# An attention and highway kernel whose engine orders come from a list instead of from ranks

## The chip, the cores and the metric

The kernel runs on one core of a Trainium2 chip. The metric is the device time of one execution in microseconds (us); the time of a kernel is the median of several runs.

## What is computed

Eight batches of twelve heads, 448 positions, 64 values a head. q and k are divided by their norms, scores are their products over tau = 0.1, a softmax follows, and the result weights v. The heads side by side are the 3584 x 768 input of a highway layer.

```
q_n = q / (norm(q) + 1e-6);  k_n = k / (norm(k) + 1e-6)
attn = softmax(q_n @ k_n.T / tau)
x = (attn @ v), heads side by side          # 3584 x 768
H = relu(x @ w_h);  T = sigmoid(x @ w_t + b_t)
out = T * H + (1 - T) * x
```

## The kernel before, in words

**The work.** A unit of attention is a *pair* of heads (n = 0 to 47, six pairs a batch); a unit of the highway layer is a *tile* of 128 rows (m = 0 to 27, three tiles a batch and a fourth for every second batch, made of what is left over of two). Each step of a pair or tile is an operation with a name, and the texts here use these names:

- `lk`, `lq`, `rk`, `rq`, `v`, `x`, `w`: loads of k, q (the main part, and the rest of 64 positions), of v (main part and rest) and of the weights. All are DMAs issued by POOL (L542 to L580, L493), and they convert to 16 bits. `f` is the first q and k, from the SP and ScalarE queues.
- `sq`, `f1`, `f2`, `red`, `nw`: squares of q and k (L602 on ScalarE or L603 on VectorE), their sums, and the inverse root in Newton steps (L631 to L636).
- `nm`: the normalised q and k of a pair, in two halves, on POOL or VectorE (L663).
- The transposed pair comes either by TensorE (`pt`, L678) and a copy (`cp`, on ScalarE L687 or VectorE L689), or by one DMA transpose on SP (`tr`, L694). 14 pairs take the first way and 34 the second.
- `qk`: scores in four parts (L734, L737), into two PSUM buffers `sc` in turn and one `sl`. `ex`: their exponentials on ScalarE (L751, L753).
- `vc`: copies of v into its padded form `vp` (ScalarE L710, VectorE L711). Two buffers `vf` hold the raw v, so the load of batch b waits for the four `vc` of batch b - 2.
- `av`: the weighted sums (L774) and `un`: the division by the sums (L782 to L788), into `xb`, and into `st` for the left-over rows, which `sh` moves to `xl` by DMA on SP.
- `xp` and `xc`, or `xt`: the transposed tile, by TensorE and a copy or by DMA on SP (10 and 18 tiles).
- `ff`: the four products of a tile (L859, bias L862). `d`, `t`, `g`, `h`, `e`, `o` are the tile's elementwise steps on VectorE and ScalarE, the last add `o` on VectorE or POOL (L946). `st0` to `st27` are the stores on SP, from three buffers.

Three PSUM buffers `pb` serve transposes, weighted sums and products alike.

**The order.** The kernel builds a list of these operations, each with the engines it may run on and a cost for each, with what it depends on, the buffers it takes and gives back. `Planner.plan` then walks through a model of time: whenever an engine is free, it takes, among the operations that are ready, the one of the lowest *step*, and so fixes engine and order. The steps are not those written beside the operations: a list `RANKS` with one number for each operation replaces them (a thousandth of the number is the step). TensorE prefers to stay with scores, or with the other matmuls, by 1.5 steps; switching costs 97 ns in the model. A load is taken only if no load of a lower step is ready. Two more lists are given: `HOLDS` says behind the scores of which pair each load is released, and `CHOICES` which of the two ways of transposing is taken. The result is a fixed instruction order for each engine. On the chip each engine works its own list from the front and waits by semaphores for what the others owe it.

[...]

The lines that pick an operation, and those that apply the lists:

```
for op in ready[e]:
    if op.when[e] > now:
        continue
    if op.dma is not None:
        if op.dma[0] == "load" and (deep or op.step > first):
            continue
...
for op, rank in zip(P.ops, RANKS, strict=True):
    op.step = rank / 1000.0
```

Of the kernel before, what the change touches and what calls it, by code (L numbers as in the profile page):

```python
# [19 lines left out]
RANKS = [  # L20
    -335, -1932, -1271, 3133, 2841, 5167, 5173, 1697, -74, 6773, 6082, 5915, 5667, -1915, -723, -495, -2732, 1644, 620, -269, 42,
    2265, -1441, -1744, 2062, 2152, -918, 3256, 2331, 4414, 3785, 5845, 5519, 4272, 2090, 6377, 10666, 9870, 9695, 10058, 9508,
    5134, 10049, 12769, 9902, 11732, 9552, 15932, 12758, 13944, 12583, 17233, 17256, 18670, 16784, 21822, 21777, 17890, 16690,
    20295, 25563, 25092, 13883, 20180, 25169, 26082, 23748, 29102, 29384, 27764, 26341, 29412, 32284, 33661, 37263, 31791, 33122,
    37907, 38585, 33898, 39108, 35328, 36704, 2394, 857, 4933, 3498, 4444, 6285, 10703, 11593, 10638, 11144, 8739, 13218, 20655,
    13960, 15171, 13417, 14400, 25150, 20593, 18723, 28847, 29728, 21766, 25308, 35536, 28630, 30992, 34871, 37517, 38415, 50453,
    45614, -1615, 1033, 685, 27, 6016, 2128, -2432, 7156, -451, -321, 1859, 3036, 2762, -1404, -5331, 5658, 8169, 4881, 6526, 927,
    11947, 3192, 4533, 3266, 11318, 7906, 9123, 8750, 15817, 13133, 9488, 11519, 13103, 13084, 13298, 13103, 15254, 13703, 13892,
    24037, 17015, 13938, 20089, 20295, 18477, 24447, 22187, 22773, 25024, 22713, 22339, 22443, 26082, 28086, 27444, 27656, 29034,
    30771, 33015, 30877, 32139, 37989, 38621, 34820, 33021, 38290, 32551, 35641, 33263, 34723, 40989, 42110, 38461, 33253, 44252,  # L30
    43633, 45447, 35798, 44076, 3231, 2565, -1751, 1566, 9632, 4904, 1466, 6198, 7375, -98991, 4914, 5920, 2537, 7720, -465, 1383,
    5460, 6251, 5748, 29126, 4663, 5087, 4744, 9779, 9843, 6545, 5105, -30262, -37170, 7855, 5855, 10788, 5142, 11144, 85225,
    8540, 7641, 9742, 4465, -114808, 7028, 11341, 12462, 7201, -37464, 10316, 9159, 13329, 10032, -121016, 12706, 8421, -78332,
    -5590, 13447, 8378, 9045, 10097, 12946, -121346, 12211, 12981, -91454, -98771, 19451, 15028, 12867, -105710, 14573, 18844,
    11133, 14125, -23135, -44370, 20938, 16676, 16656, -31575, -163611, 22258, 16377, 14459, 21437, -115592, 18504, 16397, 14004,
    13897, -88475, 19773, 16898, 18256, 57676, -91195, 15754, 19706, 22628, 22205, 21596, 10816, 18889, 18282, 201292, 45600,
    21254, 19936, 13867, 25179, -28175, 24642, 18088, 20941, -16514, 59267, 20464, 17361, 20075, 23083, 20381, -175770, 27216,
    27122, 181487, 114978, 25193, 24125, 25084, -39395, -94136, 25227, 25049, 23771, 30866, 27677, 1440, 21856, 26649, 20642,
    -93406, 25116, 22457, 23353, -5592, -73152, 27038, 25127, 26246, 26984, 28561, -147028, 33880, 30995, 68610, 33770, 31413,
    31877, 30222, -79746, 83829, 33050, 29574, 34024, 112191, 33698, 35292, 32513, 31456, -1565, 55132, 31620, 29222, 30471, 6683,  # L40
    38178, 32009, 28869, 29922, 31584, 32695, 36344, 39730, 40450, 106424, 239806, 36530, 39625, 43884, -33467, 104089, 37075,
    35523, 38187, -11090, -64566, 36130, 37728, 34352, -81003, -138719, 39693, 36458, 32804, 63129, 123831, 39266, 37892, 33195,
    108295, 133523, 37203, 45017, 41083, 41355, 108347, 44744, 40273, 39414, 11515, 194501, 41016, 41953, 42696, 48735, 37150,
    41422, 40336, 41702, 162857, 55277, 45550, 41590, 41916, 103590, 149762, 39797, 43288, 42467, 81073, 82634, 41132, 6839, 7350,
    8242, 6304, 14280, 10159, 13740, 10591, 18303, 14858, 11534, 13430, 24113, 22797, 19366, 21837, 19098, 24269, 26279, 25213,
    29363, 34108, 37459, 31510, 32869, 37287, 35777, 36518, 46146, 45644, 43305, 43543, -1403, 4599, -991, -288, 198, 4194, 3309,
    9036, 6978, 4679, 6017, 7165, 3946, 6351, 3005, 4829, 6519, 3682, 8257, 4979, 8964, 5934, 5252, 2718, 9743, 7885, 7346, 7454,
    6624, 9536, 966, 6752, 8008, 9328, 7610, 6383, 2346, 4401, 6111, 8198, 11578, 9204, 10485, 8362, 9755, 2989, 6805, 3222, 9770,
    5763, 6413, 8303, 8981, 6853, 6631, 6857, 11857, 8358, 10504, 8417, 9866, 5189, 8798, 9553, 9916, 12186, 13302, 10953, 9638,
    15284, 8840, 11922, 5831, 10408, 6315, 9449, 5527, 4622, 12082, 16809, 8219, 8672, 10011, 8092, 7049, 11942, 11705, 11157,  # L50
    12832, 15876, 7930, 9895, 9099, 5712, 10667, 13770, 11844, 9866, 11844, 12801, 10128, 15457, 14600, 15312, 14139, 17140,
    10136, 15238, 14468, 13703, 15449, 13977, 10994, 10023, 12308, 12009, 12223, 14945, 12406, 16825, 15267, 14102, 15635, 14144,
    13172, 13358, 17103, 14232, 14643, 13449, 14221, 14378, 13744, 19613, 16238, 15619, 14766, 22292, 19045, 18526, 10880, 15482,
    17749, 18298, 15280, 18728, 17528, 12279, 19524, 20449, 17979, 15834, 18591, 18055, 18938, 17702, 17919, 18780, 21066, 22200,
    19537, 14358, 18187, 22934, 19437, 18287, 21567, 15623, 20390, 21595, 17459, 16669, 17661, 17250, 18895, 16286, 18854, 20586,
    21181, 21955, 21362, 21923, 21688, 17683, 24823, 21763, 19818, 17894, 19658, 22713, 22147, 21948, 21075, 25045, 16800, 24464,
    23733, 21929, 23853, 26560, 18284, 23132, 21813, 21733, 23445, 18280, 24449, 19741, 21846, 22733, 26683, 20892, 25039, 25991,
    22326, 25330, 23979, 25318, 26442, 26729, 24225, 19280, 22262, 22552, 22093, 22645, 23788, 23923, 26924, 28536, 22788, 21384,
    23795, 22599, 26462, 27417, 26160, 25941, 24071, 26999, 25952, 25184, 27650, 31212, 27018, 26947, 28061, 27536, 28032, 29925,
    23838, 31447, 25659, 28699, 24777, 30028, 31103, 29120, 32621, 32372, 27439, 26006, 28909, 29374, 29530, 29088, 29914, 24681,  # L60
    31528, 35518, 28197, 30867, 29458, 32059, 28431, 31586, 27901, 29414, 31676, 35932, 29300, 36310, 32645, 31589, 30167, 38648,
    31605, 30849, 31730, 27814, 29997, 28249, 31468, 33782, 30279, 31438, 31179, 29456, 32630, 31483, 34201, 31369, 34151, 31355,
    34669, 33889, 36281, 32831, 36426, 35943, 30241, 30471, 30218, 31940, 36522, 35571, 35198, 32061, 36043, 35685, 34551, 34481,
    35120, 36994, 34447, 34944, 36601, 38422, 36822, 32448, 35295, 32369, 37188, 35896, 35002, 38841, 35936, 39091, 38774, 39560,
    34045, 32204, 32951, 32981, 35956, 33750, 37119, 37830, 35133, 34557, 37647, 37806, 38233, 40428, 36896, 38364, 36625, 39199,
    37755, 34740, 37385, 40737, 37549, 37703, 38412, 35577, 36947, 38983, 38392, 42624, 40461, 43990, 38941, 40965, 36940, 40435,
    42631, 39576, 39905, 42465, 39599, 39033, 40762, 40160, 43447, 43685, 39785, 38249, 42821, 40891, 39347, 43595, 41144, 45787,
    41272, 46121, 42659, 49862, 43166, 42012, 38517, 43507, 42102, 43711, 45454, 45152, 44045, 47521, 43039, 44021, 37849, 44344,
    38023, 38673, 32560, 39755, 37139, 39384, 39438, 43664, 44903, 46532, 45791, 52656, 44070, 49771, 40817, 48013, 44821, 49369,
    38608, 45378, 44257, 46036, 45379, 48187, 44122, 49724, 46123, 48526, 39822, 44757, 43950, 42745, 41717, 45307, 41257, 43609,  # L70
    49107, 46378, 42257, 43967, 41895, 44075, 42503, 46864, 46654, 51736, 48408, 49869, 47400, 50799, 45287, 48998, 45566, 51428,
    46465, 56278, 49246, 52417, 46119, 50866, 47960, 48731, 49000, 47578, 47435, 50129, 48381, 48080, 9319, 20240, 20022, 27086,
# [115 lines left out]
class Planner:  # L188
# [18 lines left out]
    def add(self, name, engs, *a, **k):  # L207
        op = Op(name, engs, *a, **k)
        op.seq = len(self.ops)
        self.ops.append(op)  # L210
        return op

    def plan(self):
        ready = {e: [] for e in ENGINES}
        self.ops = [op for op in self.ops if op.var is None or self.choices[op.var[0]] == op.var[1]]
        used = set(self.ops)
# [18 lines left out]
        mode, now = None, 0.0  # L235
# [800 lines left out]
```

## Time and profile before

| What | Value |
|---|---|
| median of five runs | 286.02 us (284.08 to 287.7) |
| the profiled execution's own time, and its span | 284.38 us, 282.6 us |
| mean granted TensorE clock | 0.956 |
| busy: TensorE, VectorE, ScalarE, POOL | 246.1, 221.9, 206.7, 130.4 us |
| transposes of q and k by DMA | 34, median 4.8 us to landing |

The span goes from the first to the last instruction; the execution's own time is 1.8 us longer. Busy times are sums over the whole span. A row of the timeline or of the waits names the line of the kernel, the operation and the tile written and read (`sc<-qkT` are scores from the transposed pair); what stands behind the arrow in brackets is what ended the idle time before it. TensorE's matmuls overlap in the pipeline, so a row's duration is longer than its share of the engine's time: a part of scores of four matmuls occupies TensorE for about 0.19 us, a weighted sum of 32 matmuls for 1.01, a product of six for 0.97 and one of seven with the bias for 1.14.

### The profile page before, as it was taken

To read this page: it belongs to the slowest core of one execution; us is meant where nothing else is said; L and a number is where in the kernel's file an instruction comes from. 1 tells how busy PE (TensorE), PEld (TensorE's weight loads), DVE (VectorE), ACT (ScalarE), POOL (GpSimd) and SP (SyncE) were. 2 spreads that over 40 slices of the span, in tenths; PEclk is the share of its full clock that TensorE was granted. 3 is DMA by queue.
4 is the path that set the end of the run, shared out by engine and by line. 5 is a ranking of instruction groups with operands and counts; after the bars stand their busy time and mean duration, and the time that the engine had idled before them with its cause. 6 is when DMAs were issued, how large, how long until landed. Compare 5 with 4: busy or idle time off the path is not lost.

```text
span 282.6 us, 7727 instructions
## 1 busy us (share of the span) xinstructions
PE 246.1 (87%) x3103; PEld 149.5 (53%) x3103; DVE 221.9 (79%) x512; ACT 206.7 (73%) x286; POOL 130.4 (46%) x170
## 2 busy tenths in 40 slices
PE   5218778999979699999998999799999999999991
PEld 1105546447635367655754566356665654676560
DVE  4588678769979977898959999599688996557663
ACT  2376986999977657999589689578899699482140
POOL 8968325766655544368570676642232240002000
PEclk9555979999999999999999999999999999999999
DMA  8999999999789999989699999999989788414823
GB/s 126 157 162 163 203 170 129 104 156 199 91 139 155 166 211 189 194 113 145 158 206 187 114 231 156 168 168 145 190 184 111 109 141 168 118 58 99 144 116 106
DMA packets 109942, 42.75 MB, mean 151 GB/s; under 512 B 103249, under 2 KB 106321, under 8 KB 109906
## 3 DMA queue, kind: packets, MB, share of 16 engines
q0 software_dynamic: 57696, 18.65, 65.5%
q1 hardware_dynamic: 51762, 23.38, 43.0%
q8 instruction: 24, 0.39, 0.6%
q10 hardware_dynamic: 448, 0.23, 0.3%
q14 instruction: 12, 0.10, 0.1%
HBM read 37.75 MB, written 11.01 MB: 173 GB/s over the span
## 4 chain that ended last, share of the span: by engine, by line
PE 56%; DMA 15%; DVE 8%; POOL 7%; ACT 6%; issue 6%; SPq 0%; DVEq 0%; ACTq 0%; POOLq 0%
PE pb L859 27%; PE pb L774 14%; PE sc L734 9%; DMA qkT<-qkn 8%; ACT ex L751 3%; DMA raw<-in_q_dram 3%; PE sl L737 3%; PE pb L862 2%; DMA raw<-in_k_dram 2%; POOL qkn L663 2%; POOL raw L560 2%; PE pb L678 2%; DMA vf<-in_v_dram 2%; POOL raw L545 1%; DVE sq L603 1%
## 5 line engine op out<-in xcount | busy, mean ns | idle before, releaser
L751 ACT ACTIVATE ex<-sc 128x896 f16<-128x896 f32 x144 | 127.3, 929 | 25.9 <-PE sc L734 25.0
L859 PEld LDWEIGHTS <-xT 128*128 128x128 f16 x672 | 61.1, 98 | 52.3 <-issue 15.0
L663 POOL TENSOR_TENSOR qkn<-raw,rs 128x448 f16<-128x448 f16 x43 | 39.8, 937 | 55.0 <-DVE rs L636 26.2
L734 PE MATMUL sc<-qkT 64*64 64x448 f16 x576 | 50.6, 378 | 15.4 <-ACT ex L751 7.1
L859 PE MATMUL pb<-w_t,xT 128*128 128x384 f16 x336 | 64.0, 327 | 0.0
L859 PE MATMUL pb<-w_h,xT 128*128 128x384 f16 x336 | 61.3, 327 | 0.9 <-DVE d L877 0.8
L774 PEld LDWEIGHTS <-ex 128*128 128x128 f16 x1536 | 53.5, 99 | 11.4 <-issue 8.2
L774 PE MATMUL pb<-vp,ex 128*128 128x65 f16 x1536 | 56.9, 195 | 1.8 <-ACT ex L751 0.7
L734 PEld LDWEIGHTS <-qkT 64*64 64x64 f16 x576 | 15.5, 106 | 36.8 <-issue 22.0
L877 DVE SCALAR_TENSOR_TENSOR d<-pb,xb 128x384 f16<-128x384 f32 x48 | 26.3, 554 | 10.9 <-PE pb L859 9.7
L663 DVE TENSOR_TENSOR qkn<-raw,rs 128x448 f16<-128x448 f16 x51 | 31.9, 664 | 0.0
L753 ACT ACTIVATE ex<-sl 128x448 f16<-128x448 f32 x48 | 26.8, 559 | 2.9 <-PE sl L737 2.9
L784 DVE TENSOR_TENSOR xb<-pb,rd 128x384 f16<-128x384 f32 x48 | 26.8, 558 | 1.7
L885 ACT ACTIVATE t<-pb 128x384 f16<-128x384 f32 x30 | 14.8, 500 | 11.1 <-PE pb L862 11.0
L885 ACT ACTIVATE pb<-pb 128x384 f32<-128x384 f32 x26 | 12.9, 498 | 13.3 <-PE pb L862 13.2
L946 POOL TENSOR_TENSOR o<-d,xb 128x768 f32<-128x768 f16 x6 | 9.8, 1636 | 27.7 <-DVE d L938 21.0
L602 ACT ACTIVATE sq<-raw 128x2688 f16<-128x2688 f16 x9 | 22.0, 2452 | 0.6 <-DMA vf<-in_v_dram 0.6
L917 DVE SCALAR_TENSOR_TENSOR pb<-pb,d 128x384 f32<-128x384 f32 x26 | 14.6, 562 | 6.8 <-ACT pb L885 6.8
L782 DVE RECIPROCAL rd<-pb 128x7 f32<-128x7 f32 x48 | 9.7, 201 | 10.9 <-PE pb L774 10.5
L862 PE MATMUL pb<-brow,ones 128*128 128x384 f16 x56 | 18.3, 326 | 0.0
L610 DVE TENSOR_TENSOR f<-sq 128x1344 f16<-128x1344 f16 (+2 forms) x17 | 14.6, 872 | 4.6 <-ACT sq L602 4.5
L737 PE MATMUL sl<-qkT 64*64 64x448 f16 x96 | 18.0, 362 | 0.1
(69 smaller groups left out, 265.3 us busy)
## 6 DMA issues: line engine op xcount, KB each, us to landing
out_dram<-o SPq DMA_DIRECT2D x24, 384.0 KB, 3.8
vf<-in_v_dram POOLq DMA_DIRECT2D x16, 288.0 KB, 6.4
raw<-in_k_dram POOLq DMA_DIRECT2D x14, 288.0 KB, 6.7
raw<-in_q_dram POOLq DMA_DIRECT2D x14, 288.0 KB, 7.3
out_dram<-o SPq DMA_DIRECT2D x8, 192.0 KB, 2.9
w_t<-in_moe_w_t_dram POOLq DMA_DIRECT2D x2, 576.0 KB, 8.8
w_h<-in_moe_w_h_dram POOLq DMA_DIRECT2D x2, 576.0 KB, 14.3
vp<-in_v_dram POOLq DMA_DIRECT2D x16, 48.0 KB, 4.7
```

What stands on the lines that cost most here:

```text
L602: return nc.scalar.square(o, r)
L663: return eng.tensor_mul(qkn_r[n][:, :, g, :], raw_r[b][:, 42 * g + 7 * hn : 42 * g + 7 * hn + 7], rs_r[b][:, g, h].unsqueeze(2).to_broadca ...
L734: last = nc.tensor.matmul(sc_r[n, j][o, g, 0:S], lhsT=T[:, 128 * j + 64 * i : 128 * j + 64 * i + 64], rhs=rhs, start=True, stop=True)
L737: nc.tensor.matmul(sl_r[n][r, 0:S], lhsT=T[:, 832:896] if g == 0 else T[:, 384:448], rhs=rhs, start=True, stop=True)
L751: nc.scalar.activation(o, sc_r[n, j][:, :, 0:S], AF.Exp, scale=inv_tau / (NSC * NSC))
L753: nc.scalar.activation(ex[:, 3136 : 3136 + S], sl_r[n][:, 0:S], AF.Exp, scale=inv_tau / (NSC * NSC))
L774: nc.tensor.matmul(u[:, s * 65 : s * 65 + 65], lhsT=l, rhs=r, start=(m == 0), stop=(m == len(ms) - 1))
L784: nc.vector.tensor_tensor(out=xo, in0=u[:, 0:6, 0:D].rearrange("p (g i) e -> p g i e", g=2), in1=rd[:, 0:6].rearrange("p (g i) -> p g i", ...
L859: nc.tensor.matmul(pt[:, 0:MH], lhsT=xT[:, c, :], rhs=w_sb[w][:, c, ms], start=(c == 0), stop=(w == 0 and c == CC - 1))
L862: nc.tensor.matmul(pt[:, 0:MH], lhsT=ones[:, :], rhs=brow[:, ms], start=False, stop=True)
L877: nc.vector.scalar_tensor_tensor(out=d_r[m][:, h], in0=pb_r[m, w, h][:, 0:MH], scalar=0.0, in1=xsrc()[:, ms], op0=ALU.max, op1=ALU.subtract)
L885: nc.scalar.activation(src if flat else t_r[m][:, h], src, AF.Tanh, scale=0.5)
```

## The change

`RANKS` goes. In its place stands `QUEUES`: for each of the five engines the numbers of the operations that it runs, in the order in which it runs them. The planner gets this list. It sets each operation to the one engine whose list names it, and in its walk through time an engine may take nothing but the front of its list, even if other operations are ready; the rule that a load waits for loads of lower steps does not apply. What the walk still decides are the buffers (which of two or three, by the model's times) and the order in which the instructions are written down. `HOLDS` has new numbers. `CHOICES`, the costs, the operations and all shapes are as before. The list was found by small moves, each judged by the end of the plan in the model.

```
-RANKS = [
-    -335, -1932, -1271, 3133, 2841, 5167, 5173, 1697, -74, 6773, 6082, 5915, 5667, -1915, -723, -495, -2732, 1644, 620, -269, 42,
...
-]
+QUEUES = {
+    "PE": [
+        1, 196, 466, 468, 470, 472, 201, 476, 478, 216, 480, 211, 506, 482, 496, 498, 206, 500, 474, 502, 486, 484, 488, 490, 492,
...
+    ],
...
+}
...
-    def plan(self):
+    def plan(self, queues=None):
...
+        if queues is not None:
+            for e in ENGINES:
+                for op in queues[e]:
+                    op.engs = {e: op.engs[e]}
+            queues = {e: list(reversed(queues[e])) for e in ENGINES}
...
-                    if op.when[e] > now:
+                    if op.when[e] > now or (queues is not None and op is not queues[e][-1]):
                         continue
                     if op.dma is not None:
-                        if op.dma[0] == "load" and (deep or op.step > first):
+                        if queues is None and op.dma[0] == "load" and (deep or op.step > first):
                             continue
...
+                if queues is not None:
+                    queues[e].pop()
...
-    for op, rank in zip(P.ops, RANKS, strict=True):
-        op.step = rank / 1000.0
...
+    queues = {e: [P.ops[i] for i in QUEUES[e]] for e in ENGINES}
...
-    order = P.plan()
+    order = P.plan(queues)
```

In operations, the fronts of TensorE's two lists read (`qk1_2` is part 2 of pair 1's scores, `ff2_00` the first product of tile 2):

```
before: fill pt0 qk0_0 qk0_1 qk0_2 qk0_3 pt1 qk1_0 qk1_1 pt4 pt3 pt2 qk1_2 qk1_3 qk4_0 av0 qk3_0 av1 qk3_1 ...
after:  fill pt0 qk0_0 qk0_1 qk0_2 qk0_3 pt1 qk1_0 qk1_1 pt4 qk1_2 pt3 qk4_0 qk1_3 qk3_0 qk3_1 pt2 qk3_2 av0 ...
```

and those of SP's:

```
before: bld f tr5 xt1 sh0 st0 st1 tr12 xt4 sh1 tr13 tr14 xt6 tr16 tr17 st2 tr15 tr18 st3 tr20 tr21 st4 tr22 ...
after:  bld f tr5 xt1 tr12 tr13 tr17 xt4 tr14 st0 sh0 st1 tr16 tr15 sh1 st2 xt6 tr18 tr20 tr21 tr22 xt7 sh2 ...
```

## The prediction

> **What bounds the kernel now.** I read the summary first, then the time cut into stretches of 20 us, then the waits, then TensorE's and ScalarE's timelines where the waits are long. The page's summary and slices:
>
> ```profile
> PE 246.1 (87%) x3103; PEld 149.5 (53%) x3103; DVE 221.9 (79%) x512; ACT 206.7 (73%) x286; POOL 130.4 (46%) x170
> ...
> PE   5218778999979699999998999799999999999991
> ...
> PEclk9555979999999999999999999999999999999999
> ```
>
> TensorE carries the kernel. Its idle time is at the front: slices 1 to 6 are thin, and the granted clock is half there. The stretches (start:end, length, then busy time and count of PE, PEld, DVE, ACT, POOL, then clock, DMA share, GB/s) say how the load is spread:
>
> ```profile
> 20.00:40.00 20.00, 13.70 (x198) 9.30 (x199) 15.38 (x34) 16.11 (x20) 9.37 (x13) 0.76 1.39 174
> 40.00:60.00 20.00, 18.50 (x234) 11.19 (x231) 15.19 (x39) 16.50 (x24) 15.19 (x19) 0.94 1.33 128
> 60.00:80.00 20.00, 17.05 (x278) 11.48 (x276) 18.69 (x45) 19.01 (x23) 11.82 (x15) 1.00 1.20 147
> 80.00:100.00 20.00, 17.39 (x165) 8.91 (x166) 17.52 (x35) 13.80 (x20) 11.88 (x14) 1.00 1.18 162
> 100.00:120.00 20.00, 19.73 (x321) 13.13 (x320) 15.52 (x36) 15.54 (x24) 7.90 (x9) 1.00 1.38 199
> ...
> 240.00:260.00 20.00, 20.00 (x296) 13.63 (x295) 11.84 (x32) 10.68 (x17) 2.34 (x2) 1.00 0.35 86
> ```
>
> After 100 us TensorE is full but for a few us; between 60 and 80 ScalarE (19.01 of 20) and VectorE (18.69) are nearly as full. An order can win only what TensorE idles. The waits of TensorE and its weight loads:
>
> ```profile
> PEld L734 <- DMA qkT<-qkn: 8.0, 6, 2.1
> PE sc L734 <- ACT ex L751: 7.1, 9, 2.4
> PE sc L734 <- DMA qkT<-qkn: 6.1, 4, 2.0
> ```
>
> So what an order can repair is in two places: scores waiting for exponentials, nearly all before 40 us, and scores waiting for a DMA transpose of q and k. The four transposes are these (TensorE's timeline; idle before in brackets):
>
> ```profile
> 80.11 0.57 PE L734 MATMUL sc<-qkT 64*64 64x448 f16 x8 [1.97 <-DMA qkT<-qkn]
> ...
> 93.02 0.38 PE L734 MATMUL sc<-qkT 64*64 64x448 f16 x4 [1.03 <-DMA qkT<-qkn]
> ...
> 99.07 0.38 PE L734 MATMUL sc<-qkT 64*64 64x448 f16 x4 [1.46 <-DMA qkT<-qkn]
> ...
> 181.85 0.57 PE L734 MATMUL sc<-qkT 64*64 64x448 f16 x8 [1.69 <-DMA qkT<-qkn]
> ```
>
> They are pairs 12, 17, 15 and 32: 6.15 us together. After 185 us no idle of TensorE is worth naming until the last matmul at 276.3, and the 6.3 us behind that are the last tile's own chain.
>
> **What changes in total.** No instruction is added to TensorE or SP, and the choice of transposing by TensorE or by DMA is the same. Counted in the two instruction orders, VectorE gets 6 more normalisations (0.664 us), 5 more value copies (0.444), 2 fewer copies of transposed q/k (0.619), 1 fewer of x (0.556) and 3 fewer final adds (0.968): 3.98 + 2.22 - 1.24 - 0.56 - 2.90 = +1.5 us. ScalarE loses 5 value copies (0.691) and gets 2 q/k copies (0.906) and one x copy (0.799): -0.8 us. POOL loses 6 normalisations (0.937) and gets 3 adds (1.636): -0.7 us. None of this decides. TensorE changes between score matmuls and the others 164 times instead of 170; the first group of six after scores takes 1.08 us in the chain and a later one 0.97, so 6 x 0.11 = **-0.7 us**, on the path.
>
> **Up to 47 us: ScalarE's list.** From 28.2 to 45.1 us ScalarE hardly idles, so its list is the path.
>
> ```profile
> 33.38 2.46 ACT L602 ACTIVATE sq<-raw 128x2688 f16<-128x2688 f16 x1
> ...
> 41.60 1.73 ACT L751 ACTIVATE ex<-sc 128x896 f16<-128x896 f32 x2 [0.85 <-PE sc L734]
> ...
> 46.64 0.91 ACT L687 COPY qkT<-pb 128x896 f16<-128x896 f16 x1 [1.58 <-PE pb L678]
> ```
>
> Two value copies of batch 0 leave it (0.70 + 0.67, less 0.1 of overlap each: 1.2). cp4 comes and cp2 goes (even). nm1_1 moves in front of the batch's last Newton step nw0_3 (1.45 us), so pt1 and cp1 come about 1 us earlier; two of the three transposes in front of qk1_2 move behind it, which takes the 1.16 us idle before ex1_2. Against that, cp0 now stands behind the 2.45 us square sq0_3: the first exponential goes from 15.5 to about 17.1, but 2.93 us of idle before cp1 hide it. If those are gone, it costs 1.6. The value loads v1 and one weight load move behind the loads of batch 1 (rk1_0 landed at 30.8 behind a weight load, and the squares need it). Then pt7 moves in front of av5, and the 1.58 us before cp7 go. Bounds for ex7_0 (48.46): 0 if tr5, which landed 11.7 us after its issue, comes no earlier (qk5_0 moves in front of qk4_2), -4 if it does. I take -2.4, nearer the copies' sum.
>
> **47 to 79 us gives part of it back.** cp8, cp10 (0.81 each net of overlap) and vc1_01 (0.60) come to ScalarE before 60 us: +2.2, so about -0.2 is left at ex9_0. The three copies of batch 2's values then leave the stretch in which ScalarE is full: -1.8. TensorE idles only some 1.5 us between 60 and 79 before the wait for pair 12, so it can't use all. I take **-1.0** for everything before 79 us; ends 0 and -2.5.
>
> **The table load.** The warm-up activation, first in ScalarE's list, moves behind cp7, and the built order shows the load of the function table behind six of the seven waits for the first q and k loads. The row: ACT_TABLE_LOAD 1,283 ns, the warm-up starting 0.02 us after it. The Trainium skill, "ScalarE: Activation LUTs", What ACT_TABLE_LOAD costs, adds a drain of 1,380 ns, 2.66 in all. The first square would start at 6.4 + 1.3 = 7.7 by the row, at 9.1 by the rule; pt0 would end at 13.3 or 14.7. Either is before the 15.6 at which sq0_3 now lets cp0 run, so it costs nothing, and 1.3 to 2.7 if cp0 were not held. By the rule sq0_1 on VectorE, behind the moved brow (1.2 us), would be 0.9 late; no drain shows in the trace, so I take 0.
>
> **The transposes.** SP's list now has tr12, tr13, tr17 in a row, ahead of stores st0, st1 and of sh0. The normalisations of pair 17 follow those of pair 12 on POOL: nw2_0 ended at 72.8, six POOL steps of 0.93 give 78.4, and with the median landing of 4.8 us tr17 is there at 83 instead of 93. tr15 is issued some 4 us earlier than its 89.4. tr12 comes no earlier, but xp3 and ff5_00 (0.45 + 0.97) move in front of qk12_0. tr32 moves ahead by one transpose and two normalisations; about 1.2 of its 1.69. Sum 1.4 + 1.0 + 1.5 + 1.2 = 5.1. The next late thing there is qk13_1, which by its place has no spare time to ex12_2; I take **-4.0**, ends 0 and -6.15. The stores cost nothing unless the three output buffers run out: st5, st3 now wait on SP behind xt7 and sh2, that is until un17 (113.6 us), and o9_0, due at 125.4, needs st3's buffer; st7 waits behind tr30, 20 us later than before. 3.8 us to land fits; at 10 us VectorE would stop in front of o9_0.
>
> **New waits.** (1) vc2_31 moves from 68.6 to behind ex15_2, about 104; it frees the buffer for v3_0, which was issued at 99.1 and landed in 8.6. Now about 105, landing at 110 to 113.7. In ScalarE's list vc3_00 stands in front of ex20_0 (was 111.83), ex18_1 and t6_0, and TensorE's next scores wait for those; in VectorE's, vc3_01 stands in front of un17. Between -0 and 2.5; most loads of this size took 4.5 to 7, so +0.8. (2) tr41 comes behind eight VectorE steps that start with un30, so at av30's end plus 4.5 (189.3 + 4.5 us), landing in 4.3 to 8.5: qk41_0 at 199.5 waits 0 to 3; +0.5. (3) tr38 is behind sh5, which waits for un35 (203.5): 205 + 4.3 to 5.6 against qk38_0 at 209.2, 0 to 2; +0.5. Together **+1.8**, ends 0 and 7.5.
>
> **Sum.** -0.7 - 1.0 - 4.0 + 1.8 = -3.9 us. The profiled execution took 284.38 (span 282.6); 280.5 then. It is 1.6 below the median of 286.02, so the median should be **282.1**. One per cent of 286 is 2.9 us, about what this kernel's measurement can tell from no change (its five runs spread over 3.6).
>
> **Rivals.** *Slower, by colliding transfers (291, chance 0.22).* The loads of batches 4 to 7 are released earlier: first k load of batch 4 behind qk4_0 instead of qk14_0, of 5 behind qk1_0 instead of qk19_0, of 6 behind qk12_0 instead of qk26_0, of 7 behind qk10_0 instead of qk31_0. If they then run beside the transposes, these land late. In the trace a transpose lands in 2.6 to 11.7 us; those beside loads are the long ones:
>
> ```profile
> DMA to landing us min/median/max: 2.6/4.8/11.7
> ```
>
> The Trainium skill, "DMA: Bandwidth & Descriptors", Queues, rings and completion order, says each DMA engine takes turns between its queues packet by packet; two queues would at most double 2.6 to an estimated 5.2, and the rival would be nothing. tr17 took 6.9 and tr15 9.7, so the row decides. Price: the waits of four batches, each 5 us longer, less some 2.5 us by which most transposes now stand ahead of their use, +10; less the 4.7 of gain, +5. It decides from 3.7 us longer (4 x 1.2 = 4.8), a median landing of 8.5 us, on. Against it: batch 4's loads would be through before tr12.
>
> *No change (286, 0.26).* ScalarE and VectorE are so full from 47 to 80 us that TensorE only waits for another engine, or the engines wait at the same places whatever the list says: gain in switches and transposes 2.5, lost again in v3, tr41 and tr38.
>
> *All of it (277.5, 0.10).* The start keeps 2.5, all four transposes go, no new wait: -0.7 - 2.5 - 5.1 = -8.3.
>
> *The forecast* has 0.42 and covers 280 to 283.5; some 0.03 of it lies within 1%. Chances: faster by over 1% 0.39 + 0.10 = 0.49, within 0.26 + 0.03 = 0.29, slower 0.22. The range for 8 in 10 is 277 to 290.5; the forecast's own is 280 to 283.5.
>
> **What would show it.** In the profile after: ex7_0 near 46 us; no wait for a transpose at pairs 17 and 15; vc3_00 or vc3_01 with an idle time before it on a value load; the table load behind the first loads; median landing of the transposes. I am wrong if that median is above 8.5, or if TensorE between 47 and 80 us idles more than 4 us.

## The result and the profile after

The changed kernel takes 284.35 us in the median of 43 runs (280.53 to 288.33). The kernel before, run beside it and in the comparisons since, takes 285.49 (80 runs, 282.62 to 290.38). The ratio is 0.993, with a 95% interval of 0.991 to 0.995: a gain that is clear of the spread, but of 0.7% or 2.0 us, where 3.9 were forecast. The ratio leaves out the runs that lie over 1.5% above the fastest of their kernel; the two medians of all runs are 1.1 us (0.4%) apart. The profiled execution took 285.21 us (span 283.4), so it shows no gain of its own; it is read here for where time was won and where it was lost again.

The page's summary and slices of the changed kernel:

```profile
PE 247.7 (87%) x3103; PEld 150.2 (53%) x3103; DVE 222.6 (79%) x517; ACT 206.2 (73%) x284; POOL 130.0 (46%) x167
...
PE   4138799999999199999999799999999899999991
...
PEclk9555999999999869999999999999999999999998
```

The thin slices at the front are fewer than before, but a new hole stands in slice 14, with TensorE at one tenth, and the granted clock falls behind it. The stretches of 20 us, in the columns explained with the prediction, show the same:

```profile
20.00:40.00 20.00, 16.22 (x245) 9.93 (x246) 17.72 (x43) 18.07 (x24) 14.19 (x20) 0.78 1.26 150
...
60.00:80.00 20.00, 18.95 (x250) 11.40 (x249) 18.42 (x46) 18.28 (x23) 11.87 (x13) 1.00 1.03 131
80.00:100.00 20.00, 13.76 (x124) 6.84 (x121) 13.36 (x28) 11.29 (x18) 7.20 (x8) 0.93 1.29 175
100.00:120.00 20.00, 19.95 (x293) 12.85 (x293) 16.00 (x37) 15.88 (x24) 11.73 (x14) 0.90 0.94 96
```

From 20 to 80 us TensorE is busy for longer in every stretch: 16.22 against 13.70, 19.56 against 18.50, 18.95 against 17.05. From 80 to 100 it has 13.76 instead of 17.39, and for the next 20 us it works at a mean clock of 0.90. Of the waits on transposes, these are left (the changed kernel's list of waits: in total, times, longest):

```profile
PEld L857 <- DMA xT<-xl: 8.9, 3, 6.4
...
PE pb L857 <- DMA xT<-xl: 6.0, 1, 6.0
```

The second line and the longest of the three waits in the first (6.4) are the same wait, once as TensorE's matmul and once as its weight load. It isn't for a pair's q and k any more, but for `xT<-xl`, the DMA transpose of a tile made of left-over rows. The waits for transposed q and k, matmuls and weight loads together, fell from 14.2 us in 10 waits to this (the changed kernel's transposed pairs):

```profile
  DMA qkT<-qkn: 2.3, 4
...
DMA to landing us min/median/max: 2.6/3.4/7.7
```

How far ahead or behind the changed kernel is at a given piece of work follows from the starts of the same operations in the two traces (us):

| operation | before | after | ahead by |
|---|---|---|---|
| ex1_2 | 27.37 | 25.88 | 1.49 |
| ex4_1 | 38.53 | 35.48 | 3.05 |
| ex7_0 | 48.46 | 42.67 | 5.79 |
| ex9_0 | 59.28 | 56.32 | 2.96 |
| qk12_0 | 80.11 | 75.17 | 4.94 |
| ff6_00 | 100.72 | 98.12 | 2.60 |
| qk20_0 | 111.34 | 111.31 | 0.03 |
| ff13_00 | 161.05 | 162.66 | -1.61 |
| qk32_0 | 181.85 | 179.97 | 1.88 |
| ff27_11 | 273.03 | 273.87 | -0.84 |

So 5 us are ahead when the scores of pair 12 start, and nothing is left at pair 20. (Rows of this table are for finding the place; where an operation itself was moved in its list, its row shows that too. qk32_0, for one, now stands ahead of ff14_00.) This is where it goes (TensorE's timeline):

```profile
91.78 0.33 PE L860 MATMUL pb<-brow,ones 128*128 128x384 f16 x1
98.12 2.10 PE L857 MATMUL pb<-w_h,xT 128*128 128x384 f16 x6 [6.01 <-DMA xT<-xl]
```

ff6_00, the first product of tile 6, is ready to start at 92 and gets its operand at 98.1. SP's timeline shows why:

```profile
81.09 2.69 SPq L692 DMA_TRANSPOSE qkT<-qkn  x2
83.83 1.23 SPq L805 DMA_DIRECT2D xl<-st  x2
...
91.89 1.21 SPq L825 DMA_TRANSPOSE xT<-xl  x1
```

The `xl<-st` is sh1, the left-over rows of the second batch in two copies, behind tr16 and tr15. It is issued at 83.83. The transpose xt6, which reads what it moved, is issued only at 91.89, when sh1 has landed: 8.0 us. xt6 then needs 6.2 more. The kernel before did the same two steps in 2.4 and 2.8 us:

```profile
79.30 1.22 SPq L807 DMA_DIRECT2D xl<-st  x2
...
83.44 1.21 SPq L827 DMA_TRANSPOSE xT<-xl  x1
```

What runs beside them in the changed kernel stands on POOL's timeline:

```profile
80.82 1.64 POOL L944 TENSOR_TENSOR o<-d,xb 128x768 f32<-128x768 f16 x1 [4.17 <-DVE d L936]
82.40 0.89 POOL L543 DMA_DIRECT2D raw<-in_q_dram  x1
...
85.58 0.85 POOL L570 DMA_DIRECT2D vf<-in_v_dram  x1
```

Five loads of batch 4 leave in 4 us (lq4_0_0 and v4_0 are shown; rk4_0, lq4_0_1 and lk4_0_1 stand between them): four of 288 KB and one of 48 KB, 1.2 MB. The last one lands at 97.3. In the kernel before the same five were spread from 85.5 to 107.5. Four loads of batch 4 left close together there too (from 85.5 to 90.0, three of 288 KB), but sh1 had landed by then and xt6 did at 86.2, and it was tr17 (86.1 to 93.0) and tr15 (89.4 to 99.0) that landed late. The hypothesis for the experiments is that these loads make sh1 and xt6 late, and that it is the new order on SP which leaves sh1 and xt6 to meet them.

### The profile page after: what moved, and what is told of

It is laid out like the page before. It is cut to its first block, busy times and chain, and to the rows that moved or that the text cites. A ratio compares the mean times of both kernels' runs of the same rounds, so it can differ in the third digit from the quotient of the medians.

```text
span 283.4 us, 7673 instructions
## 1 busy us (share of the span) xinstructions
PE 247.7 (87%) x3103; PEld 150.2 (53%) x3103; DVE 222.6 (79%) x517; ACT 206.2 (73%) x284; POOL 130.0 (46%) x167
## 4 chain that ended last, share of the span: by engine, by line
PE 55%; DMA 16%; DVE 11%; POOL 7%; ACT 5%; issue 2%; SPq 0%; DVEq 0%; POOLq 0%; ACTq 0%
PE pb L857 30%; PE pb L772 13%; PE sc L732 8%; DMA vp<-in_v_dram 4%; ACT ex L749 3%; DMA xT<-xb 3%; PE pb L860 2%; PE sl L735 2%; POOL raw L543 2%; DMA xT<-xl 2%; DMA w_t<-in_moe_w_t_dram 2%; DMA out_dram<-o 2%; POOL raw L558 2%; DMA vf<-in_v_dram 2%; DMA qkT<-qkn 2%
## 5 line engine op out<-in xcount | busy, mean ns | idle before, releaser
L857 PE MATMUL pb<-w_h,xT 128*128 128x384 f16 x336 | 63.0, 332 | 8.2 <-DMA xT<-xl 6.0
L772 PEld LDWEIGHTS <-ex 128*128 128x128 f16 x1536 | 52.9, 98 | 10.1 <-issue 8.2
L661 POOL TENSOR_TENSOR qkn<-raw,rs 128x448 f16<-128x448 f16 x37 | 34.7, 951 | 39.6 <-issue 17.3
L944 POOL TENSOR_TENSOR o<-d,xb 128x768 f32<-128x768 f16 x9 | 14.7, 1637 | 53.6 <-DVE d L936 25.5
L661 DVE TENSOR_TENSOR qkn<-raw,rs 128x448 f16<-128x448 f16 x57 | 35.3, 653 | 0.0
L732 PEld LDWEIGHTS <-qkT 64*64 64x64 f16 x576 | 16.3, 106 | 28.3 <-issue 18.7
L608 DVE TENSOR_TENSOR f<-sq 128x1344 f16<-128x1344 f16 (+2 forms) x17 | 14.2, 837 | 7.9 <-ACT sq L600 7.7
L578 POOL DMA_DIRECT2D vp<-in_v_dram x16 | 11.1, 695 | 19.8 <-PE sc L732 18.6
```

What stands on the lines that cost most here:

```text
L661: return eng.tensor_mul(qkn_r[n][:, :, g, :], raw_r[b][:, 42 * g + 7 * hn : 42 * g + 7 * hn + 7], rs_r[b][:, g, h].unsqueeze(2).to_broadca ...
L732: last = nc.tensor.matmul(sc_r[n, j][o, g, 0:S], lhsT=T[:, 128 * j + 64 * i : 128 * j + 64 * i + 64], rhs=rhs, start=True, stop=True)
L772: nc.tensor.matmul(u[:, s * 65 : s * 65 + 65], lhsT=l, rhs=r, start=(m == 0), stop=(m == len(ms) - 1))
L857: nc.tensor.matmul(pt[:, 0:MH], lhsT=xT[:, c, :], rhs=w_sb[w][:, c, ms], start=(c == 0), stop=(w == 0 and c == CC - 1))
```

## The experiments

Every kernel below is the changed kernel with the edit shown. Lists are given by the names of operations; the edits are in `QUEUES` and, where said, in `HOLDS`.

**The left-over rows first.** The three DMAs of tile 6's path go to about where the kernel before had them.

```
-SP: ... xt1 tr12 tr13 tr17 xt4 tr14 st0 sh0 st1 tr16 tr15 sh1 st2 xt6 tr18 ...
+SP: ... xt1 sh0 tr12 tr13 tr17 xt4 sh1 tr14 xt6 st0 st1 tr16 tr15 st2 tr18 ...
```

> The kernel after, with three entries of SP's list moved: sh0 behind xt1, sh1 behind xt4, xt6 behind tr14. Theory A (SP's order): in the kernel after, sh1 and xt6 stand behind transposes and stores, meet the burst of batch 4's loads (sh1 8.0 us to land, xt6 6.2) and hold TensorE 6.2 us at the first product of tile 6; moved, xt6 lands before 86 us, this wait is gone and with it the fall of the granted clock behind it (0.93 and 0.90 in the two stretches from 80 to 120 us), and the time falls by 6 to 9 us against the kernel after: 275 to 278. Rival B (the lead can't be kept): tr15, which landed at 90.3, or the exponentials of pair 15 are late next and TensorE waits there instead; the time stays within 2 us of 284.

Measured: 283.17 us (20 runs), ratio 0.9916 (0.9887 to 0.9945) to the 285.46 of before beside it, which can't be told from the changed kernel's 0.993. xt6 now leaves at 80.9 and lands at 83.7. But the transposes behind it now meet the loads, which leave from 83.3 on. SP's timeline, and then TensorE's:

```profile
83.27 3.36 SPq L692 DMA_TRANSPOSE qkT<-qkn  x2
```

```profile
95.45 0.59 PE L732 MATMUL sc<-qkT 64*64 64x448 f16 x4 [4.49 <-DMA qkT<-qkn]
```

tr16 takes 7.1 us and tr15, issued at 85.2, takes 10.2. TensorE stands still for pair 15 instead of tile 6. The lateness isn't a matter of tile 6's path; whatever is issued beside the loads pays. The 275 to 278 us of the first theory were missed for that reason; what came is its rival B.

**The loads behind xt6.** SP's list stays as the change has it, and the five loads stand behind the next normalisation on POOL.

```
-POOL: ... nm15_0 o2 lq4_0_0 rk4_0 lq4_0_1 lk4_0_1 v4_0 nm18_1 rq4_1 ...
+POOL: ... nm15_0 o2 nm18_1 lq4_0_0 rk4_0 lq4_0_1 lk4_0_1 v4_0 rq4_1 ...
```

> The kernel after, with SP's list untouched and five entries of POOL's list (lq4_0_0, rk4_0, lq4_0_1, lk4_0_1, v4_0) moved behind nm18_1, so that they are issued after about 94 us and not at 82 to 86. Theory A' (contention): with no loads beside them sh1 lands in 2.5 to 3.5 us instead of 8.0 and xt6 in 3 to 4.5 instead of 6.2, so xt6 is there at about 91 and the 6.2 us wait nearly goes: 277 to 281. Rival C (the place in SP's list alone): sh1 and xt6 land as late as before, 284. If the loads then come too late, the squares of batch 4 wait and VectorE or ScalarE show it after 105 us.

Measured: 286.26 us (20 runs), ratio 1.0016 (0.9984 to 1.0049). With the loads gone from there, sh1 takes 4.0 us instead of 8.0, and xt6 2.7 instead of 6.2; the stretch from 80 to 100 is whole. SP's timeline:

```profile
83.76 1.23 SPq L805 DMA_DIRECT2D xl<-st  x2
...
87.88 1.21 SPq L825 DMA_TRANSPOSE xT<-xl  x1
```

The loads now leave from 94.2 on, and the next transpose that meets them is tr20 (99.9 to 109.3). The stretch behind 100 us and TensorE's timeline of this kernel:

```profile
100.00:120.00 20.00, 13.16 (x160) 7.61 (x161) 13.04 (x23) 10.21 (x16) 11.08 (x13) 0.83 1.46 141
```

```profile
109.31 0.96 PE L732 MATMUL sc<-qkT 64*64 64x448 f16 x8 [6.62 <-DMA qkT<-qkn]
```

This shows the cause of the late sh1 and xt6, and also that holding the loads back doesn't help: the wait moves with them, at its full size.

**SP's front as before.** The first 18 operations of SP's list in the order that the kernel before had.

```
-SP: bld f tr5 xt1 tr12 tr13 tr17 xt4 tr14 st0 sh0 st1 tr16 tr15 sh1 st2 xt6 tr18 ...
+SP: bld f tr5 xt1 sh0 st0 st1 tr12 xt4 sh1 tr13 tr14 xt6 tr16 tr17 st2 tr15 tr18 ...
```

> The kernel after, with the first 18 entries of SP's list (to tr18) in the order of the kernel before; all else as after. It undoes the gain that the prediction put at 3.9 us for pairs 12, 17 and 15 and brings back the early xt6. If the transposes' order is worth what was predicted, waits for pairs 17 and 15 of 1 to 2.5 us each come back while the 6.2 us wait for xt6 goes: net 2 to 4 us faster than the kernel after, 280 to 282. If the transposes' order is worth nothing (they were early because TensorE and POOL were early), it is as fast as with only sh0, sh1 and xt6 moved, 275 to 278.

Measured: 280.05 us (4 runs), ratio 0.9841 (0.9757 to 0.9924). sh1 and xt6 are through before the loads (xt6 79.1 to 81.8); tr15 alone meets them, 84.2 to 93.1. That leaves one wait:

```profile
93.17 0.38 PE L732 MATMUL sc<-qkT 64*64 64x448 f16 x4 [1.80 <-DMA qkT<-qkn]
```

The front of SP's new list takes away about as much as the whole change gives: with that part undone the kernel is 1.6% faster than before (0.8 to 2.4), instead of 0.7%.

**Everything that is needed ahead of the loads.** If only those DMAs suffer that are in flight beside the loads, an order that issues all of them before the loads leave should have no wait at all.

```
-SP: bld f tr5 xt1 tr12 tr13 tr17 xt4 tr14 st0 sh0 st1 tr16 tr15 sh1 st2 xt6 tr18 ...
+SP: bld f tr5 xt1 sh0 st0 st1 tr12 xt4 sh1 tr13 tr14 tr17 xt6 tr15 tr16 st2 tr18 ...
```

> The kernel after, with the first 18 entries of SP's list in a third order: sh0, st0, st1 in front of tr12 and sh1 behind xt4, as before; then tr13, tr14, tr17, xt6, tr15, tr16, st2, tr18. Theory T: the wait near 95 us is made by a burst of five loads of batch 4 (1.2 MB) that POOL issues together at 82 to 87, because o2 holds its list until 81; whichever transposes SP has in flight then land 5 to 10 us late. Here tr17, xt6 and tr15 are all issued before about 82 us, and tr16, in the burst, is not needed before 100: TensorE waits less than 1 us in all for transposes between 80 and 100 us, and the time is 277 to 280, below the 280.05 of the run with the front of before. Rival B (the lead can't be kept): another engine's result is late next in the same stretch, TensorE idles there as long as before, 280 to 284.

Measured: 278.53 us (4 runs), ratio 0.9805 (0.9752 to 0.9858) to the 284.68 of before beside it. SP's timeline, then the stretch:

```profile
77.38 3.95 SPq L692 DMA_TRANSPOSE qkT<-qkn  x3
81.50 1.21 SPq L825 DMA_TRANSPOSE xT<-xl  x1
```

```profile
80.00:100.00 20.00, 20.00 (x235) 11.25 (x233) 19.28 (x43) 17.44 (x27) 9.02 (x11) 1.00 0.98 148
```

From tr13 to tr16 every transpose lands 2.6 to 2.8 us after its issue, the loads leave together as ever, from 85.3 to 88.4, and TensorE doesn't idle between 80 and 100. Only SP's list was edited, and the lists of the other engines are the same (the planner then gives some operations another of their two or three buffers), so this is the measure of what the changed order lost there. TensorE's list from ff6_00 to qk20_0 is the same in both: it takes 10.56 us here (94.46 to 105.02) and 13.19 in the changed kernel (98.12 to 111.31). The same list takes 10.56 in each of the three other kernels here in which TensorE doesn't stop in it or just before it (SP's front as before, the add behind the loads, the best version). So the stop costs twice: 6.0 us of waiting, and 2.6 more for the work behind it. The reason for the second part stands in the changed kernel's stretches of 2 us: the granted clock is 0.50 from about 97 to 104.

```profile
98.00:100.00 2.00, 1.88 (x6) 0.74 (x6) 0.00 (x0) 0.00 (x0) 0.00 (x0) 0.50 0.34 68
...
104.00:106.00 2.00, 2.00 (x41) 1.25 (x40) 1.47 (x3) 0.72 (x2) 0.96 (x2) 1.00 1.20 177
```

At qk20_0 the two kernels are 6.3 us apart and at the last product 5.65, although at qk12_0 this one is 2.9 behind (78.03 against 75.17). Why it is behind there is not shown; the kernel with two loads held (next), whose SP list is the changed kernel's, was 1.1 behind at that place too.

**Two loads held.** lk4_0_1 and v4_0 wait for the scores of pair 15; the lists stay.

```
-HOLDS: lk4_0_1 12, v4_0 10
+HOLDS: lk4_0_1 15, v4_0 15
```

> The kernel after, with all five lists untouched and two release points changed: lk4_0_1 and v4_0 are released behind the first scores of pair 15 (about 90 us) and not behind those of pairs given in the kernel after. Theory T: the burst at 82 to 86 is three loads and not five, sh1 lands at about 88 and not at 91.8, xt6 at 91 to 93 and not at 98.1, and the wait of 6.2 us at tile 6 falls to 0 to 2: 279 to 281.5. Theory A (SP's order alone makes it): sh1 and xt6 are as late as before, and the time is 284. Rival (the same bytes collide wherever they go): the two loads meet tr18 or tr20, and a wait of 4 to 7 us stands at pair 18 or 20, as when all five were moved; 284 to 286.

Measured: 283.14 us (4 runs), ratio 0.989 (0.9796 to 0.9983). Beside three loads sh1 still takes 6.7 us (84.9 to 91.6), and xt6, issued at 91.7, meets the two that were held (issued at 91.7 and 92.5) and takes 5.7:

```profile
97.45 2.10 PE L857 MATMUL pb<-w_h,xT 128*128 128x384 f16 x6 [4.68 <-DMA xT<-xl]
```

The expected fall of the wait, to 0 to 2 us, was missed. Taking two loads out of the group isn't enough, since three suffice to delay these copies of 48 KB almost as much as five (6.8 to 8.0 in three traces), and the held two meet xt6.

**The add behind the loads.** In the changed kernel o2, which ran on VectorE before, stands in front of the five loads on POOL and waits for VectorE until 80.8. Is it what sends them off together?

```
-POOL: ... nm15_0 o2 lq4_0_0 rk4_0 lq4_0_1 lk4_0_1 v4_0 nm18_1 ...
+POOL: ... nm15_0 lq4_0_0 rk4_0 lq4_0_1 lk4_0_1 v4_0 o2 nm18_1 ...
```

> One edit to the changed kernel: on POOL the add o2 (1.64 us, it waits for h2 of VectorE until 80.8) moves behind the five loads lq4_0_0, rk4_0, lq4_0_1, lk4_0_1, v4_0, which stand behind it there. Nothing is left out. Theory O (it is o2 that turns the five loads into a burst): lq4_0_0 and the loads behind it start near 76.7, when nm15_0 ends, are spread, and the wait for xt6 falls below 2 us; the median 279 to 282. Rival H (the release of rk4_0 behind the scores of pair 14, which begin at 81.3, holds the list just as long): lq4_0_0 goes at 76.7, the other four still leave in a row from 81.4 to 85, sh1 still lands later than 90 and xt6 later than 96; the wait stays at 4 to 7 us and the median at 283 to 286.

Measured: 285.5 us (10 runs), ratio 1.0034 (0.9983 to 1.0085). POOL's timeline:

```profile
77.15 0.89 POOL L543 DMA_DIRECT2D raw<-in_q_dram  x1
85.31 0.66 POOL L558 DMA_DIRECT2D raw<-in_k_dram  x1 [7.27 <-PE sc L732]
```

One load goes early, and the other four leave in a row from 85.31 on, behind rk4_0, which is held for the scores of pair 14. So the theory of the add falls: with or without it, the in-order list and that hold let the loads go together. (That an earlier release of rk4_0 would spread them was not tried.) The early load alone made tr14 6.2 us long (77.7 to 84.0), and o2, now late, held VectorE:

```profile
90.14 0.56 DVE L782 TENSOR_TENSOR xb<-pb,rd 128x384 f16<-128x384 f32 x1 [4.38 <-POOL o L944]
```

TensorE waited in two other places:

```profile
84.01 0.38 PE L732 MATMUL sc<-qkT 64*64 64x448 f16 x4 [2.10 <-DMA qkT<-qkn]
...
90.88 2.08 PE L857 MATMUL pb<-w_h,xT 128*128 128x384 f16 x6 [3.69 <-DVE st L786]
```

Together 5.8 us, as much as the wait for tile 6 that is gone; only its place was not foreseen.

**The early loads as before.** v1_0 and w10 go back in front of the second half of batch 0's value rests (x0_1), v1_1 in front of the first load of batch 2.

```
-POOL: ... lq1_0_0 x0_0 rk1_0 rk1_1 w11 x0_1 w01 nm5_1 lk2_0_0 ...        -HOLDS: v1_0 3, v1_1 5
+POOL: ... lq1_0_0 v1_0 x0_0 rk1_0 rk1_1 w11 w10 x0_1 w01 nm5_1 v1_1 lk2_0_0 ...  +HOLDS: v1_0 0, v1_1 1
```

> The kernel after, with three entries of POOL's list near where they stood in the kernel before: v1_0 behind lq1_0_0, w10 behind w11, v1_1 ahead of lk2_0_0 (1.15 MB of loads that come before the first half of the kernel needs them), released as before. Theory L: the lead of 5.8 us that the kernel after has at ex7_0 (42.7 against 48.5) comes to a good part from these loads standing later, by which tr5 landed 4.1 us after its issue and not 11.7, and the squares of batch 1 had their data earlier; with them back, tr5 lands in 8 to 12 us and ex7_0 is at 45 to 48. Rival: the lead comes from the orders of ScalarE and TensorE alone (copies that left, pt7 ahead of av5), and ex7_0 stays at 42 to 44.

Measured, a single run: 286.1 us. tr5 lands in 9.7 us (4.0 in the changed kernel, 11.7 before) and ex7_0 starts at 48.22, so the lead of the start is gone. But most of it goes in a way that the kernel before did not have. TensorE's timeline:

```profile
34.72 1.09 PE L772 MATMUL pb<-vp,ex 128*128 128x65 f16 x17 [4.93 <-DMA vp<-in_v_dram]
```

x0_1 was issued at 25.3 and landed at 34.7, behind w10 and v1_0. In the kernel before it left together with x0_0 and landed at 27.4. So the run shows what a load in front of a needed one costs (5.5 us at ex7_0, and 5.6 us of landing time for tr5), but it doesn't divide the start's 5.8 us between the loads and ScalarE's order. ff6_00 came 3.2 us later than in the changed kernel, after a wait for xt6 of 4.2 us instead of 6.0. That doesn't show that some of the lead was worth nothing: in the next kernel, which keeps most of the lead, the same wait was 4.3. With the same lists on SP and POOL around it, this wait differs by 1.7 us from trace to trace.

**The table load first.** The warm-up activation goes back to the front of ScalarE's list.

```
-ACT: sq0_0 sq0_3 cp0 ... cp7 warm ex7_0 ...
+ACT: warm sq0_0 sq0_3 cp0 ... cp7 ex7_0 ...
```

> The kernel after, with the warm-up activation first in ScalarE's list, as before. The prediction said that the table load behind the first loads costs nothing. By the trace after it delays nm0_1 and, through brow, sq0_1 (14.15 instead of 13.17). If that is the path, f10_3 starts at the end of sq0_3 and pt1 comes 0.6 us earlier than 20.95; if sq0_3 sets it, pt1 stays at 20.9. Either way the time changes by less than a single run can tell.

Measured, a single run: 280.52 us, at the lower edge of the changed kernel's own runs, so it decides nothing on the total. pt0 starts at 11.96 instead of 13.14 and pt1 at 20.17 instead of 20.95, but ex7_0 at 43.55 instead of 42.67. The load in its new place costs 1.2 us at pt0 and 0.8 at pt1, and none of it is left at ex7_0. In the best version (next), beside the kernel without this edit, pt0 gains 1.1 again but pt1 only 0.1, so the 0.8 is not firm. Why the rest of the start came later with it was not pursued.

**The best version.** The SP front that had no wait, the table load first, and in SP's list sh3 and xt13 ahead of st8 and st9 (tile 13 had waited 2.3 us for its left-over rows in the changed kernel).

> The kernel e5_transposes_before_burst, and with it the warm-up activation first in ScalarE's list (pt1 came 0.8 us earlier when that was changed alone) and sh3 and xt13 in front of stores st8 and st9 (the wait of 2.1 us for xt13 at 162 us). Theory T: 0.5 to 2.5 us below e5_transposes_before_burst, 275.5 to 279, the fastest of all. If the first 20 us and the wait at tile 13 are covered by the next late thing, it is within 0.5 us of e5_transposes_before_burst.

Measured: 277.53 us (6 runs), ratio 0.9753 (0.9706 to 0.98). This is the fastest of all, 2.5% below the kernel before and, by the two ratios, 1.8% below the changed one. It is 1.0 us under the version with the SP front alone, whose interval overlaps with its own; the two further edits aren't shown to be worth anything. The wait at tile 13 had nothing left to give: in the trace of the version with the SP front alone ff13_00 waited only 0.02 us. In the trace of the best version, too, ex7_0 comes later with the table load first (44.16).

## Why the prediction was right or wrong

**The start: right in kind, too small.** 2.4 us were taken up to ex7_0, "nearer the copies' sum", with -4 as the end. It was 5.8, beyond even that end; part of it is order, since pt7 now stands ahead of av5, and behind the same work (all to pt7 and av5) TensorE goes on at 42.17 instead of 46.44, 4.3 ahead. The table of starts gives the terms: 3.05 at ex4_1, put down here to the copies and the transposes moved; 1.7 more at ex5_0 (36.87 against 41.60), where the idle time before that line is gone; 0.9 at cp7, and 0.2 at ex7_0. ScalarE's timeline after, to set beside the three lines shown of before:

```profile
29.54 2.49 ACT L600 ACTIVATE sq<-raw 128x2688 f16<-128x2688 f16 x1
...
36.87 1.73 ACT L749 ACTIVATE ex<-sc 128x896 f16<-128x896 f32 x2
...
41.01 0.91 ACT L685 COPY qkT<-pb 128x896 f16<-128x896 f16 x1
```

All three idle times named in the prediction went (1.16, 0.85, 1.58), and tr5 landed in 4.0 us, although issued 2.6 later. The step that failed is the choice between the ends: the sums were there, and tr5's part was left out because its landing couldn't be told from the order.

**47 to 79 us: given back on ScalarE, but not on TensorE.** With the added copies the lead at ex9_0 is 2.8 us smaller (5.79 to 2.96); 2.2 were forecast. TensorE lost none of its lead: ff2_10, behind the same work in both lists, starts at 70.46 instead of 75.38, which is 4.9 ahead where 1.0 was forecast for everything before 79 us. The excess is the start's.

**The table load: right in the end.** 0 at ex7_0. The reason given, that sq0_3 holds cp0 for as long, covered pt0; pt1 came 0.8 or 0.1 later for it. For the drain of the Trainium skill ("ScalarE: Activation LUTs", What ACT_TABLE_LOAD costs) the trace shows nothing: the load takes 1.28 us at 6.84, and the square starts at 8.14.

**The transposes: right, and more.** 4.0 of 6.15 us were taken. At pair 12 0.55 us of waiting are left, and at 17, 15 and 32 no matmul waits for a transpose: 5.6 us. (The rival that takes all four counts 5.1 for them; they are 6.15.)

**The new waits: the step that was wrong.** The +1.8 for v3, tr41 and tr38 didn't come. No copy of values waits for its load, and pairs 38 and 41 start with TensorE busy. What came is +6.0 at tile 6, and 2.6 behind it. In the prediction this is the sentence "The stores cost nothing unless the three output buffers run out": it looked at what lies on SP behind the transposes for buffers only. That tr12, tr13 and tr17 stand ahead of sh0 was written down, and not followed to its reader; that sh1 and xt6 were moved behind tr16 and tr15 was not written at all, although ff6_00 reads them. Where a list is in order, every entry that is moved back needs its reader named.

The search that made the list was blind at the same place. In the planner's model, worked out from the kernel's file, sh1 lands 3.1 us after its issue and xt6 4.8 (8.0 and 6.2 in the trace), and the plan of the changed kernel ends 1.7 us ahead of that with everything needed ahead of the loads (263.2 and 264.9 us), where the chip has it 5.8 behind.

**The rival of colliding transfers** had the mechanism and a wrong measure. It was to decide by the median landing of the q and k transposes, from 8.5 us on; the median fell from 4.8 to 3.4. What matters is which few DMAs are in flight in the 15 us of one group of loads. The one argument against the rival, "batch 4's loads would be through before tr12", was read from the release of the first load alone: lk4_0_0 did leave at 67.2, but rk4_0 is held for the scores of pair 14, and the three loads behind it in POOL's list can't pass it. The prediction set the rule of the Trainium skill ("DMA: Bandwidth & Descriptors", Queues, rings and completion order), taking turns between queues packet by packet, from which it drew at most a doubling to an estimated 5.2 us (its own inference; the section states no such bound), against the row, and let the row decide. That was right: beside these loads single transposes took 6.2 (xt6), 9.4 (tr20 with the loads held) and 10.2 us (tr15 with the left-over rows first), against 2.6 to 2.8 clear of them.

**The sum.** The 0.7 us for fewer switches can't be told apart in these traces. 4.94 us are gained to pair 12, and 0.03 are left at pair 20: 6.0 lost at tile 6 and 2.6 behind it, less 3.7 which the waits for the transposes of 12, 17 and 15 bring in between (xp3 and ff5_00 are done by qk12_0 in the new list, so the wait for pair 12 is not yet in the 4.94). Tile 13 loses 1.64 more (its left-over rows again), pair 32 gains its 1.69, and a product at 222.21 waits 0.92 for VectorE: 0.03 - 1.64 + 1.69 - 0.92 = -0.84, the last line of the table. The wait at tile 13 as TensorE's weight load has it:

```profile
162.66 1.74 PEld L857 LDWEIGHTS <-xT 128*128 128x128 f16 x12 [2.29 <-DMA xT<-xl]
```

These are the terms of one execution, a slower one than the median; in the two other traces with the same lists around tile 6 the stop was 4.2 and 4.3 us. Over all runs 2.0 are gained. The sign held, but that the total came within 2.3 us of the forecast is luck: the time before 79 us and the transposes brought some 5 us more than was taken (4.9 for 1.0, and 5.6 for 4.0), and stops that weren't foreseen took more than that back (6.0, 2.6, 1.64 and 0.92 for 1.8). When ff6_00 was ready but for its operand, at about 92, the changed kernel was 8.8 us ahead of the kernel before (100.72); a gain of the size of the rival "all of it" was there, and most of it was given back in one place. With that place mended the median is 278.5.

## What to carry to other kernels

In a fixed in-order list, take every DMA that is moved back, name its reader, and look at what else is in flight between its issue and its landing. A group of loads that one held entry lets go together was here a time in which hardly any small DMA was quick: issue what the next 15 us need ahead of the group. Holding all of the loads, or two of the five, only gave the wait to the next reader. And a plan is only as good as its model: where the model lets a DMA land in 3 us and the trace shows 8, the list that it finds best is not.

## What the runs showed of the hardware

Two 48-KB copies between on-chip buffers (sh1) took 2.4 us clear of loads (by the one landing in the trace of before), 4.0 beside a store and transposes, 6.7 beside three loads and 6.8 to 8.0 beside five, so the delay doesn't grow in step with the bytes. With a single 288-KB load in flight, tr14 took 6.2 us instead of 2.7. A stop of TensorE of 6.0 us had an after-effect of 2.6: the granted clock was 0.50 for about 7 us, from some 5 us after the stop began, and the first product in it took 2.10 us instead of 1.14. In all these traces the stops of 3.7 us and more after 40 us (seven traces) were followed by such a stretch at 0.50, and those of up to 2.1 us were not.
